# Spreading a column of maxima over all rows: one fp32 matmul, or three bf16 matmuls over the words of its bits

## The chip, the cores and the metric

The kernel runs on one core of a Trainium2 chip. The metric is the device time of one execution in microseconds (us): the median of several runs. Beside the runs there is one profiled execution of the kernel before, with a trace of every instruction; its span and its waits are what this document reads.

Five engines work side by side, each on its own list of instructions in order: TensorE (PE, with its weight loads on PEld), VectorE (DVE), ScalarE (ACT), GpSimd (POOL) and SyncE (SP), which issues the transfers.

## The reference

Linear attention over 8 batches, 8 heads, 576 positions and head size 64, and then a gated feed-forward network with an RMS norm over the 4608 tokens of width 512:

```python
def _attn_ref(q, k, v):
    q_s = softmax of q over the head dimension          # exp(q - max), over its sum
    k_s = k - np.max(k, axis=2, keepdims=True)          # maximum over the 576 positions
    k_s = np.exp(k_s)
    k_s = k_s / (np.sum(k_s, axis=2, keepdims=True) + 1e-09)
    kv = np.einsum('bhsd,bhse->bhde', k_s, v)
    return np.einsum('bhsd,bhde->bhse', q_s, kv)

def _moe_ref(x, w_gate, w_val, w_out, rms_g):           # x: 4608 x 512
    xn = x / rms * rms_g
    g = xn @ w_gate                                     # 512 x 1536
    return (g * sigmoid(g) * (xn @ w_val)) @ w_out
```

What matters here is the maximum of k over the positions: 64 numbers for each batch and head, or 128 for each pair of heads. There are 8 batches and 4 pairs, so 32 such columns of 128 maxima.

## The kernel before

The tokens are done in nine blocks of 512. The attention of later blocks runs between the matrix products of the feed-forward network of earlier ones. The order of all work is written out by hand: a string `ORDER` holds some 3000 steps such as `k_max.5.2` or `pp.3.1.6`; a loop calls the function of each name with its numbers, and each engine gets its instructions in the order in which these calls issue them. There is no scheduler behind it. A letter after a colon (`:D`, `:A`, `:P`) chooses the engine of a step that can run on several.

For a batch `b` over 0 and a pair of heads `g`, the steps around the change are these.

- `kd_load` fetches k with the head dimension in the partitions (`kd`, 128 x 576), and `k_max` (DVE, L548) reduces it to a column `kx` of 128 maxima, one in each partition.
- `k_rows` (PE, L560) makes a 128 x 128 tile in PSUM whose every row holds the 128 maxima: the column `kx`, repeated 128 times, is the stationary operand, and the identity matrix `ident` is the moving one, both fp32. The trace shows an fp32 matmul as two passes, each with a weight load of its own (28 matmuls of this kind are 56 records).
- `k_sub` (DVE, L565) subtracts that tile from k with the positions in the partitions (`kt`), and `k_exp` (ACT, L573) takes the exponential.
- `k_mm` (PE, L600) multiplies it by v: ten fp32 matmuls of 64 x 65, which are 20 records.
- `k_eps`, `k_rec`, `kv_hi`, `kv_lo` (DVE, DVE, ACT, DVE; L628, L631, L388, L651) divide by the sums and split the result into two parts for `q_x` (PE, L796).

For batches 2 to 7, one step `k_seg` holds two of these: it takes one PSUM bank (pool `ps_a`, two banks), does `k_mm` of one pair of heads and then `k_rows` of the next, so that on PE the ten matmuls of L600 stand straight ahead of the one of L560. There are 25 such steps; the first has only `k_rows`, the last only `k_mm`. For batch 1 the four `k_rows` stand alone. For batch 0 the maxima are used along the partitions (`k_exp` takes them as its bias), and nothing is spread.

The rest of PE's work is the feed-forward network, with weights and activations split into two halves: `pp` (L1166, f16, 256 columns each), `fu` and `f2` (L1214 and L1301, mostly f16, 512 columns), `f1` and `f1p` (L1230 in fp32r words, 512 columns; L1246 in f16). `ev` (L1181, L1184, L1187, L1190 and copies in L383) empties their PSUM banks on DVE and ACT. `fill` and `warm` (L476, L470) are matmuls on constants that keep PE busy; the weights of L476 are one bf16 zero in each partition, repeated 128 times.

Of the kernel before, what the change touches and what calls it, by code (L numbers as in the profile page):

```python
# [40 lines left out]
conv_low.2.0.2 q_x0.0.1 k_load.1.1 q_max0.1.0 q_t0.0.2 x_sq.0.1 x_hi.0.1:D q_load0.1.1 q_sub0.1.0:P q_c0.0.2:A
n_sum0.1 x_lo.0.1 q_load0.1.2 v_ones.1.0 q_exp.1.0 q_x0.0.2 k_sub.1.0 k_load.1.2 v_ones.1.1 f1.0.1.0.1 q_sum0.1.0
conv_mul.1.1 f1.0.1.0.3 f1.0.0.0.1 load_w.5.0 f1.0.0.0.3 x_hi.0.2:D x_sq.0.2 k_exp.1.0 conv_shift.1.1 fill.1 n_sum0.2
conv_sign.1.1 f1.0.1.0.2 f1.0.0.0.2 conv_low.0.2.1 f1.0.0.1.0 x_lo.0.2 f1.0.1.1.0 w_hi.1.0.2:P load_w.5.1 f1.0.1.1.1
conv_mul.0.2 f1.0.0.1.1 k_max.1.1 n_sum0.3 conv_low.4.0.2 conv_shift.0.2 kd_load.1.2 f1.0.0.1.2 f1.0.0.1.3 f1.0.1.1.2
conv_sign.0.2 f1.0.0.2.0 f1.0.1.1.3 w_lo.1.1:P f1.0.1.2.0 f1.0.1.2.1 n_t.0 conv_mul.2.0 load_w.4.2 f1.0.1.2.2
f1.0.0.2.1 f1.0.0.2.2 n_y0.0 conv_one.2.0 w_lo.1.0:P f1.1.0 conv_shift.2.0 n_y1.0 conv_mul.2.1 conv_sign.2.0:P
load_w.6.0 conv_low.5.0.2 f1.0.1.2.3 conv_shift.2.1 f1.0.0.2.3 k_mm.1.0 conv_sign.2.1 f1.1.1 v_load.1.2 n_cols.0
w_hi.2.0.2:A load_w.6.1 k_load.1.3 k_max.1.2 conv_low.4.2.1 w_lo.2.0:P q_max0.1.1 kd_load.1.3 conv_mul.1.2 n_rows.0
q_sub0.1.1:P g_mul.0 conv_shift.1.2 f1.2.0 w_lo.2.1:P silu.0 conv_sign.1.2 conv_low.6.0.2 v_ones.1.2 h_mul.0  # L50
# [25 lines left out]
v_ones.1.3 h_lo.5:P n_sq.1.0 n_col.0.1 w_hi.9.0.2:A h_lo.6:P k_mm.1.2 n_max.0.1 k_rows.1.3 n_sq.1.1 k_eps.1.2
v_load.2.0 f1.8.0 k_rec.1.2 w_lo.9.1:P k_sub.1.3 k_load.2.1 kv_norm0.1.2:A k_exp.1.3 n_bits.0.1.0 q_eps0.1.3
q_rec0.1.3 w_lo.9.0:P k_mm.1.3 g_mul.8 q_mul0.1.3:P silu.7 q_t0.1.1 k_eps.1.3 k_rec.1.3 f1.8.1 silu.8 q_c0.1.1:D
kv_norm0.1.3:A h_mul.7 n_bits.0.1.1 n_bits.0.1.2 n_bits.0.1.5 w_sc.0.1 n_bits.0.1.3 n_bits.0.1.4 q_x0.1.1 h_mul.8
w_hi.10.0.2:P b_hi.0.2:A n_col.1.0 w_sc.0.0 k_max.2.0 f1.9.0 n_max.1.0 kd_load.2.1 x_sq.1.1 x_raw.1.1:D b_lo.0.2:P  # L80
# [5 lines left out]
q_sub.2.0:D o_hi.9:A f2.8 h_lo.9:D x_sq.1.3 o_lo.9:D x_raw.1.3:A x_acc.1.3:D n_bits.1.3.1 n_hi.1:A t_op.0.1:P f2.9
k_max.2.1 o_hi.10:A n_lo.1:D kd_load.2.2 n_bits.1.3.3 o_lo.10:P q_exp.2.0 n_sum.1 q_sum.2.0 o_hi.11:A t_op.0.2:P
k_seg.0 q_half2.2.0 f1.10.0 n_t.1 v_ones.2.1 o_lo.11:P n_y0.1 n_y1.1 t_op.0.3:P f1.10.1 t_lo.0.0:P g_mul.10 n_rows.1
silu.10 t_hi.0.1:P q_half.2.1 f1.11.0 h_mul.10 x_nrm.1.1:P k_max.2.2 h_hi.10:A k_sub.2.0 kd_load.2.3 h_lo.10:P
# [1293 lines left out]
```

## Time and profile before

| what | value |
|---|---|
| runs before | 933.83 us median of 3 (933.64 to 934.41) |
| the profiled execution | 932.69 us, span 930.9 us from the first to the last instruction |
| PE | 913.8 us busy, 98% of the span |
| DVE | 617.3 us, 66% |
| ACT | 559.1 us, 60% |
| POOL | 305.9 us, 33% |
| granted TensorE clock | 1.0 |

A page of the profile gives the busy time of each engine, and the chain of work that ended last: from the last instruction back to whatever released it, or to the instruction before it on its engine. Matmuls are pipelined and overlap in the records, so "busy" for PE means that some matmul is under way, not that none waits; the steps from one start to the next say more than the durations. A line number (L560) is a line of the kernel before.

### The profile page before, as it was taken

How to read it: one execution, taken by the hardware profiler on the slowest of the kernel's cores; microseconds unless marked ns; L12 is line 12 of the kernel's file. 1: busy time of each engine (PE TensorE's matmuls, PEld its weight loads, DVE VectorE, ACT ScalarE, POOL GpSimd, SP SyncE). 2: the span in 40 equal slices, each digit the busy share in tenths (PEclk: the TensorE clock that was granted, in tenths of full speed). 3: DMA queues.
4: the chain of work that ended last, by engine and by line, in shares of the span. 5: the costliest groups of instructions: out<-in, count | busy, mean ns of one | idle time of the engine just before them, and what ended most of it. 6: DMA issues, size and time to landing. Idle time of an engine off the chain costs nothing.

```text
span 930.9 us, 16383 instructions
## 1 busy us (share of the span) xinstructions
PE 913.8 (98%) x6479; PEld 644.0 (69%) x6479; DVE 617.3 (66%) x1330; ACT 559.1 (60%) x880; POOL 305.9 (33%) x304
## 2 busy tenths in 40 slices
...
GB/s 342 360 265 226 61 53 38 36 23 188 54 53 131 33 42 24 110 94 53 66 117 77 65 53 29 36 51 1 38 35 23 1 2 46 1 1 24 23 1 46
DMA packets 29550, 68.06 MB, mean 73 GB/s; under 512 B 3744, under 2 KB 4000, under 8 KB 29472
## 3 DMA queue, kind: packets, MB, share of 16 engines
...
q14 instruction: 27, 0.22, 0.1%
HBM read 57.55 MB, written 9.44 MB: 72 GB/s over the span
## 4 chain that ended last, share of the span: by engine, by line
PE 83%; DVE 6%; ACT 4%; DMA 3%; issue 2%; POOL 1%; SPq 0%; ACTq 0%; POOLq 0%; DVEq 0%
PE ps_gv L1166 38%; PE ps_o L1214 22%; PE ps_o L1301 5%; PE ps_gv L1230 5%; PE ps_gv L1246 4%; PE ps_a L796 2%; PE ps_a L600 2%; DMA qt<-in_q_dram 1%; PE ps_a L560 1%; DMA w_gv<-in_kt_dram 1%; DMA w_br<-in_w_dram 1%; PE ps_a L1021 1%; ACT w_gv L388 0%; PE ps_a L725 0%; DVE x_raw L827 0%
## 5 line engine op out<-in xcount | busy, mean ns | idle before, releaser
L1166 PEld LDWEIGHTS <-w_gv 128*128 128x128 f16 x2016 | 196.0, 98 | 39.7 <-issue 3.2
L1166 PE MATMUL ps_gv<-xo,w_gv 128*128 128x256 f16 x1296 | 155.8, 273 | 0.6 <-ACT w_br L383 0.4
L1166 PE MATMUL ps_gv<-x_op,w_gv 128*128 128x256 f16 x720 | 86.5, 273 | 0.2
L1166 PEld LDWEIGHTS <-w_br 128*128 128x128 f16 x756 | 73.7, 98 | 14.3 <-issue 1.3
L1214 PEld LDWEIGHTS <-hh 128*128 128x128 f16 x504 | 48.9, 98 | 49.8 <-issue 0.4
L1214 PEld LDWEIGHTS <-hl 128*128 128x128 f16 x504 | 49.0, 98 | 47.5 <-issue 0.6
L1214 PE MATMUL ps_o<-w_o,hl 128*128 128x512 f16 x336 | 79.9, 379 | 0.0
L1214 PE MATMUL ps_o<-w_o,hh 128*128 128x512 f16 x336 | 78.4, 379 | 0.0
L1230 PE MATMUL ps_gv<-xo,wf 128*128 128x512 f32 x264 | 66.7, 404 | 0.0
L1166 PE MATMUL ps_gv<-xo,w_br 128*128 128x256 f16 x540 | 66.1, 273 | 0.0
L1230 PEld LDWEIGHTS ps_gv<-xo,wf 128*128 128x128 f32 x264 | 49.0, 188 | 12.9 <-issue 2.8
L1166 PEld LDWEIGHTS <-wf 128*128 128x128 f16 x504 | 49.2, 98 | 8.1 <-issue 0.3
L1181 DVE TENSOR_TENSOR tm<-ps_gv,tm 128x512 f32<-128x512 f32 x29 | 20.0, 689 | 50.9 <-PE ps_gv L1166 47.7
L785 POOL TENSOR_TENSOR ql<-qT,qh 128x512 fp32r<-128x512 f32 x14 | 18.2, 1301 | 87.1 <-ACT qh L383 87.1
L383 ACT COPY ps_gv<-ps_gv 128x512 f32<-128x512 f32 x42 | 24.0, 572 | 36.3 <-PE ps_gv L1166 13.8
L1181 DVE TENSOR_TENSOR w_br<-ps_gv,w_br 128x512 f32<-128x512 f32 x29 | 20.0, 690 | 37.4 <-PE ps_gv L1166 36.8
L1166 PE MATMUL ps_gv<-xo,wf 128*128 128x256 f16 x360 | 43.9, 273 | 0.0
L897 POOL TENSOR_TENSOR acc<-acc,sq 128x512 f32<-128x512 f32 x11 | 14.0, 1270 | 71.8 <-ACT sq L893 71.8
L1246 PE MATMUL ps_gv<-x_op,w_br 128*128 128x512 f16 x144 | 31.9, 379 | 0.0
L383 ACT COPY w_br<-ps_gv 128x512 f32<-128x512 f32 x29 | 17.0, 585 | 23.5 <-PE ps_gv L1166 23.4
L970 POOL TENSOR_TENSOR wf<-w_gv,wf 128x512 fp32r<-128x512 f32 x22 | 28.1, 1293 | 6.7 <-ACT wf L383 6.3
L383 ACT COPY tm<-ps_gv 128x512 f32<-128x512 f32 x29 | 17.0, 585 | 21.5 <-PE ps_gv L1166 21.3
...
## 6 DMA issues: line engine op xcount, KB each, us to landing
...
```

The source lines that it names most:

```text
L383: (e.copy if e is nc.scalar else e.tensor_copy)(dst, src)
L600: nc.tensor.matmul(ps[h * D:(h + 1) * D, :n1], lhsT=ke[:n, h, j], rhs=vt_[b, g][:n, j, h], start=(j == 0), stop=(j == len(rows) - 1))
L785: on(nc.gpsimd).tensor_tensor(out=ql, in0=qT_[j, g], in1=qh_[j, g][0].bitcast(F32), op=ALU.subtract)
L796: nc.tensor.matmul(px[:, c0:c1], lhsT=wt, rhs=mv[:, c0:c1], start=(i == 0), stop=(i == 2))
L897: on(nc.gpsimd).tensor_tensor(out=acc_[j], in0=acc_[j], in1=sq_[j, g], op=ALU.add)
L970: on(nc.gpsimd).tensor_tensor(out=cut(wl[:, a]), in0=W(s, a), in1=cut(wh[:, a].bitcast(F32)), op=ALU.subtract)
L1166: nc.tensor.matmul(pair(ps, i), lhsT=a[:, wt], rhs=y if i else y.rearrange("p (a c) -> p a c", a=2), start=(first and k == 0 and i == 0 an ...
L1181: nc.vector.tensor_tensor(out=v, in0=bank[j, u, 5 if n == 5 else 3], in1=v, op=ALU.add)
L1214: nc.tensor.matmul(po[2 * n + t], lhsT=a[:, o:o + P], rhs=w, start=(u == 0 and i == 0 and p == 0), stop=(u == NU - 1 and i == 1 and p == 2))
L1230: nc.tensor.matmul(pd[s], lhsT=m[:, a, c * P:(c + 1) * P], rhs=X[j, c][x], start=(n == 1), stop=(n == 3 * NKT))
L1246: nc.tensor.matmul(pd[s], lhsT=w[:, wt], rhs=x, start=(c == 0 and p == 0), stop=(c == NKT - 1 and p == 2))
L1301: nc.tensor.matmul(po[t], lhsT=a[:, t * P:(t + 1) * P], rhs=w, start=(i == 0 and n == 0), stop=(i == NF - 1 and n == len(terms) - 1))
```

## The change

`kx` becomes three columns instead of one. A new step `k_split`, called straight after `k_max` for each batch over 0, forms two remainders on DVE: the second column is the first less the number that its own upper 16 bits make as a bf16 word, and the third is the second less the upper word of the second. `upper` reads every other 16-bit word of an fp32 tile, starting with the second. `k_rows` then makes three matmuls that add up in the same PSUM tile: the upper words of each column, repeated 128 times, times the upper words of the identity, which are 1.0 and 0.0 in bf16. No other step is moved.

```diff
     def k_max(b, g):
-        kx_[b, g] = small.tile([P, 1], F32, name="kx")
-        nc.vector.tensor_reduce(out=kx_[b, g], in_=kd_[b, g], axis=AX.X, op=ALU.max, negate=b == 0)
+        t = small.tile([P, 3], F32, name="kx")
+        kx_[b, g] = [t[:, i:i + 1] for i in range(3)]
+        nc.vector.tensor_reduce(out=kx_[b, g][0], in_=kd_[b, g], axis=AX.X, op=ALU.max, negate=b == 0)
+
+    def upper(t):
+        return t.bitcast(BF16)[:, 1::2]
+
+    def k_split(b, g):
+        x = kx_[b, g]
+        for i in range(2):
+            nc.vector.tensor_tensor(out=x[i + 1], in0=x[i], in1=upper(x[i]), op=ALU.subtract)
...
     def k_rows(b, g, t=None):
         mb = (own(attn_ps(False)) if t is None else t)[:KP, P:2 * P]
-        nc.tensor.matmul(mb, lhsT=kx_[b, g].broadcast_to([P, KP]), rhs=ident, start=True, stop=True)
+        for i, x in enumerate(kx_[b, g]):
+            nc.tensor.matmul(mb, lhsT=upper(x).broadcast_to([P, KP]), rhs=upper(ident), start=i == 0, stop=i == 2)
...
-            nc.scalar.activation(kd_[b, g], kd_[b, g], AF.Exp, bias=kx_[b, g], accum_out=rs_[b, g])
+            nc.scalar.activation(kd_[b, g], kd_[b, g], AF.Exp, bias=kx_[b, g][0], accum_out=rs_[b, g])
```

In `ORDER`, 28 steps are added, each straight behind its `k_max` (the first and the last of them):

```diff
-v_load.1.1 kv_norm0.0.2:A k_max.1.0 w_hi.0.0.2:P
+v_load.1.1 kv_norm0.0.2:A k_max.1.0 k_split.1.0 w_hi.0.0.2:P
...
-kv_lo.6.3 k_max.7.3 pp.5.1.2
+kv_lo.6.3 k_max.7.3 k_split.7.3 pp.5.1.2
```

New lines shift the numbers: L560 of the kernel before is L574 after, L600 is L614, L1166 is L1180, L548 is L553, and the subtraction of `k_split` is L561.

What PE runs in one of the joint steps (`k_seg`, here the one that makes the rows of batch 3's last pair), between two products of the feed-forward network. Before (`vt` and `kt` are v and the exponentials of k, `w_gv` and `w_bx` weights):

```order
L1166 MATMUL ps_gv<-xo,w_gv 128x256
L600 MATMUL ps_a<-vt,kt 64x65 x10
L560 MATMUL ps_a<-ident,kx 128x128
L1166 LDWEIGHTS w_bx
L1166 MATMUL ps_gv<-xo,w_bx 128x2x128
```

After:

```order
L1180 MATMUL ps_gv<-xo,w_gv 128x256
L614 MATMUL ps_a<-vt,kt 64x65 x10
L574 LDWEIGHTS kx
L574 MATMUL ps_a<-ident,kx 128x128
L574 LDWEIGHTS kx
L574 MATMUL ps_a<-ident,kx 128x128
L574 LDWEIGHTS kx
L574 MATMUL ps_a<-ident,kx 128x128
L1180 LDWEIGHTS w_bx
L1180 MATMUL ps_gv<-xo,w_bx 128x2x128
```

One matmul in fp32, which loads its weights itself and runs in two passes, has become three pairs of weight load and matmul in bf16, in the same place.

What DVE runs around the maxima of batch 5, pair 2 (`qt` is a part of q, `x_raw` the attention's output). Before:

```order
L651 SCALAR_TENSOR_TENSOR kv_lo_113<-ps_a,rs,kv_hi_112 64x64 x2
L745 TENSOR_TENSOR st<-st,sw 128x16
L748 TENSOR_TENSOR qt<-qt,st 128x512
L548 TENSOR_REDUCE kx<-kd 128x1
L390 TENSOR_SCALAR x_raw<-ps_a,g_103 128x512
L897 TENSOR_TENSOR acc<-acc,sq 128x512
```

After:

```order
L665 SCALAR_TENSOR_TENSOR kv_lo_113<-ps_a,rs,kv_hi_112 64x64 x2
L759 TENSOR_TENSOR st<-st,sw 128x16
L762 TENSOR_TENSOR qt<-qt,st 128x512
L553 TENSOR_REDUCE kx<-kd 128x1
L561 TENSOR_TENSOR kx<-kx 128x1 x2
L394 TENSOR_SCALAR x_raw<-ps_a,g_103 128x512
L911 TENSOR_TENSOR acc<-acc,sq 128x512
```

Two subtractions of one element per partition stand between the maximum and the evacuation of `x_raw`, and each waits for the instruction before it, whose result it reads.

What DVE runs around the maxima of batch 1, pair 3, where the weights of the first blocks are put together from their words (L456 and L464, `w_o`). Before:

```order
L1269 TENSOR_TENSOR tm<-ps_o,tm 128x512
L548 TENSOR_REDUCE kx<-kd 128x1
L456 SCALAR_TENSOR_TENSOR ps_a<-ps_a,w_o 128x512
L464 SCALAR_TENSOR_TENSOR w_o<-w_o,ps_a 128x512
L565 TENSOR_TENSOR kt<-kt,ps_a 128x640
L694 TENSOR_REDUCE sm<-qt 128x8
```

After:

```order
L1283 TENSOR_TENSOR tm<-ps_o,tm 128x512
L553 TENSOR_REDUCE kx<-kd 128x1
L561 TENSOR_TENSOR kx<-kx 128x1 x2
L460 SCALAR_TENSOR_TENSOR ps_a<-ps_a,w_o 128x512
L468 SCALAR_TENSOR_TENSOR w_o<-w_o,ps_a 128x512
L579 TENSOR_TENSOR kt<-kt,ps_a 128x640
L708 TENSOR_REDUCE sm<-qt 128x8
```

Again the same order, with the two subtractions pushed in between. The lists of ACT, POOL and SP hold the same instructions in the same order as before.

More of the change, by code (lines that the diff above doesn't have):

```diff
@@ L41 @@
[L41 to L50, printed above, removed]
@@ L76 @@
[L76 to L80, printed above, removed]
@@ L86 @@
[L86 to L89, printed above, removed]
+k_tr0.1.0 v_load.1.0 kv_norm0.0.3:A k_tr0.1.1 conv_sign.0.1 n_sum0.0 v_load.1.1 kv_norm0.0.2:A k_max.1.0 k_split.1.0
@@ new lines @@
+w_lo.9.1:P k_sub.1.3 k_load.2.1 kv_norm0.1.2:A k_exp.1.3 n_bits.0.1.0 q_eps0.1.3 q_rec0.1.3 w_lo.9.0:P k_mm.1.3
+g_mul.8 q_mul0.1.3:P silu.7 q_t0.1.1 k_eps.1.3 k_rec.1.3 f1.8.1 silu.8 q_c0.1.1:D kv_norm0.1.3:A h_mul.7 n_bits.0.1.1
+n_bits.0.1.2 n_bits.0.1.5 w_sc.0.1 n_bits.0.1.3 n_bits.0.1.4 q_x0.1.1 h_mul.8 w_hi.10.0.2:P b_hi.0.2:A n_col.1.0
+w_sc.0.0 k_max.2.0 k_split.2.0 f1.9.0 n_max.1.0 kd_load.2.1 x_sq.1.1 x_raw.1.1:D b_lo.0.2:P b_hi.0.3:A b_hi.0.0:A
+x_acc.1.1:D n_sq.1.2 n_col.1.1 f1.9.1 b_lo.0.0:D v_ones.2.0 k_load.2.2 n_sq.2.2 n_max.1.1 w_lo.10.0:P g_mul.9 n_sq.2.0
@@ new lines @@
+b_lo.0.3:D q_t0.1.2 q_max2.2.0 w_lo.10.1:D n_sq.2.1 q_load.2.2 n_col.2.0 f2.5 t_op.0.0:D silu.9 n_max.2.0
+w_hi.11.0.2:P n_sq.3.0 h_mul.9 q_c0.1.2:D b_hi.0.1:A t_hi.0.0:A q_t0.1.3 b_lo.0.1:D n_col.2.1 h_hi.7:A v_load.2.1 f2.6
+n_max.2.1 w_lo.11.0:P n_sq.3.1 o_hi.7:A q_max.2.2 h_lo.7:P q_x0.1.2 o_lo.7:D h_hi.8:A o_hi.8:A w_lo.11.1:D f2.7
+x_sq.1.2 o_lo.8:D q_c0.1.3:A h_lo.8:D x_raw.1.2:A n_bits.1.3.0 x_acc.1.2:D q_x0.1.3 h_hi.9:A q_sub.2.0:D o_hi.9:A f2.8
+h_lo.9:D x_sq.1.3 o_lo.9:D x_raw.1.3:A x_acc.1.3:D n_bits.1.3.1 n_hi.1:A t_op.0.1:P f2.9 k_max.2.1 k_split.2.1
@@ new lines @@
+v_ones.2.2 q_load.3.0 k_rec.2.1 q_sub.2.2:P k_sub.2.2 kv_hi.2.1:A k_load.3.0 v_load.2.3 h_mul1.18 t_op.1.3:P k_exp.2.2
+k_max.3.1 k_split.3.1 q_exp.2.2 h_hi.18:P k_seg.3 kv_lo.2.1 kd_load.3.2 q_sum.2.2 q_x.2.0 h_lo.18:P k_load.3.1
+k_sub.2.3 silu1.19 v_load.3.0 f2.16 q_hi.2.1:A k_eps.2.2 q_half2.2.2 v_ones.2.3 t_op.2.1:P x_sq.2.0 q_half.2.3
+x_raw.2.0:A k_rec.2.2 q_max2.2.3 kv_hi.2.2:A q_sum2.2.2 q_rec.2.2 q_sub.2.3:P kv_lo.2.2 f2.17 q_max.3.0 q_mul.2.2:P
+k_max.3.2 k_split.3.2 q_exp.2.3 q_lo.2.1:P k_exp.2.3 kd_load.3.3 q_sum.2.3 q_x.2.1 q_half2.2.3 v_ones.3.0 t_op.2.2:P
@@ new lines @@
+q_t.2.2 k_seg.4 x_sq.2.1 q_half.3.0 q_load.3.1 t_op.2.3:P q_hi.2.2:A k_eps.2.3 f2.18 k_rec.2.3 v_load.3.1 k_sub.3.0
+x_raw.2.1:A k_load.3.2 q_lo.2.2:P kv_hi.2.3:A k_max.3.3 k_split.3.3 k_exp.3.0 kv_lo.2.3 kd_load.4.0 x_acc.2.1:P
+q_max.3.1 q_x.2.2 k_seg.5 q_sum2.2.3 v_ones.3.1 x_sq.2.2 q_rec.2.3 t_lo.0.3:P x_raw.2.2:D f1p.19.1 v_load.3.2
+k_eps.3.0 k_rec.3.0 q_mul.2.3:P k_sub.3.1 k_load.3.3 t_hi.1.0:A kv_hi.3.0:A k_max.4.0 k_split.4.0 x_acc.2.2:P
+k_exp.3.1 q_t.2.3 kd_load.4.1 f1p.20.0 h_mul1.19 t_lo.1.0:P q_hi.2.3:A q_load.3.2 kv_lo.3.0 h_hi.19:A q_lo.2.3:D
@@ L193 @@
-hu_lo.3.5.1:P k_rec.5.2 k_sub.5.3 kv_hi.5.2:A pp.4.0.2 ev.4.0.2 kv_lo.5.2 q_sum2.6.0 q_rec.6.0 q_mul.6.0:D pp.4.0.7
-ev.4.0.8 v_ones.6.0 k_max.6.2 pp.4.0.5 ev.4.0.3 kd_load.6.3 pp.4.0.4 ev.4.0.5 k_exp.5.3 pp.4.0.3 q_exp.6.1 q_sum.6.1
-q_x.5.2 ev.4.0.6 ev.4.0.9 k_seg.16 ev.4.0.10 x_sq.5.2 ev.4.0.11 pp.4.1.1 v_load.6.1 hu_hi.4.0.0 x_acc.5.2:D k_load.6.2
+kv_lo.4.2 pp.3.2.6 ev.3.2.8 q_max2.5.2 q_sub.5.2:D k_max.5.2 k_split.5.2 q_x.4.2 ev.3.2.2 v_ones.5.0 pp.3.2.5
+x_raw.4.2:D q_hi.4.3:A kd_load.5.3 x_sq.4.2 q_lo.4.3:P pp.3.2.7 x_acc.4.2:D fu.3.1.1.0 k_exp.4.3 q_t.5.0 ev.3.2.3
@@ new lines @@
+q_load.5.3 k_seg.12 q_exp.5.2 ev.3.2.5 q_sum.5.2 pp.3.2.3 v_load.5.1 k_eps.4.3 k_load.5.2 k_rec.4.3 k_sub.5.0
+kv_hi.4.3:A fu.3.1.1.1 ev.3.2.6 k_exp.5.0 ev.3.2.10 pp.3.3.1 v_ones.5.1 kv_lo.4.3 hu_hi.3.2.0 q_half2.5.2
+hu_lo.3.2.0:P fu.3.1.0.0 q_max.5.3 q_half.5.3 fu.3.1.0.1 q_sum2.5.2 q_rec.5.2 q_mul.5.2:D fu.3.2.0.0 q_max2.5.3
+q_sub.5.3:D k_max.5.3 k_split.5.3 q_exp.5.3 pp.3.2.4 q_sum.5.3 kd_load.6.0 q_x.4.3 q_half2.5.3 ev.3.2.9 fu.3.2.0.1
+q_sum2.5.3 x_raw.4.3:D x_sq.4.3 ev.3.2.11 ev.3.3.0 k_seg.13 x_acc.4.3:D hu_hi.3.2.1 pp.3.3.6 k_eps.5.0 k_load.5.3
@@ new lines @@
+o_x_lo.4.5:P q_hi.5.2:A pp.3.5.2 x_raw.5.1:D hu_lo.3.4.0:P q_max.6.1 pp.3.5.6 o_x_hi.4.6:A k_max.6.1 k_split.6.1
+q_lo.5.2:P ev.3.5.8 kd_load.6.2 fu.3.4.1.1 ev.3.5.2 o_x_lo.4.6:D pp.3.5.5 q_t.5.3 x_sq.5.1 q_max2.6.0 q_load.6.2
+x_acc.5.1:D pp.3.5.7 q_sub.6.0:D k_exp.5.2 fu.3.4.0.0 ev.3.5.3 q_exp.6.0 ev.3.5.5 fu.3.4.0.1 q_sum.6.0 q_half2.6.0
+pp.3.5.3 q_max.6.2 q_half.6.1 pp.3.5.4 ev.3.5.6 ev.3.5.10 pp.4.0.1 ev.3.5.9 q_max2.6.1 q_sub.6.1:D hu_hi.3.5.0
+k_seg.15 ev.3.5.11 ev.4.0.0 hu_lo.3.5.0:D hu_hi.3.5.1 pp.4.0.6 v_load.6.0 k_eps.5.2 k_load.6.1 hu_lo.3.5.1:P k_rec.5.2
@@ L298 @@
-fu.8.4.0.0 store.8.3 fu.8.4.0.1 fu.8.5.0.0 fu.8.5.0.1 store.8.0 store.8.1
+q_sum2.6.1 q_rec.6.1 q_mul.6.1:D q_x.5.3 k_max.6.3 k_split.6.3 q_exp.6.2 pp.4.1.4 ev.4.1.5 kd_load.7.0 x_sq.5.3
+q_sum.6.2 x_raw.5.3:A x_acc.5.3:P pp.4.1.3 q_half2.6.2 k_exp.6.0 q_half.6.3 fu.3.5.1.1 n_hi.5:A ev.4.1.6 n_lo.5:P
+store.3.2 pp.4.2.1 store.3.3 ev.4.1.10 n_sum.5 q_max2.6.3 hu_hi.4.1.0 q_sub.6.3:D k_seg.17 q_hi.6.0:A hu_lo.4.1.0:D
+q_exp.6.3 fu.4.0.0.0 v_load.6.2 n_t.5 q_lo.6.0:P k_load.6.3 n_y0.5 fu.4.0.1.0 n_y1.5 ev.4.1.9 fu.4.0.1.1 ev.4.2.0
@@ new lines @@
+pp.4.4.7 q_rec.7.0 k_max.7.1 k_split.7.1 v_ones.6.3 q_mul.7.0:P kd_load.7.2 q_x.6.1 ev.4.4.3 q_sum2.6.3 q_rec.6.3
+q_mul.6.3:D pp.4.4.4 q_hi.6.2:A q_max.7.1 x_raw.6.1:A q_lo.6.2:P q_half.7.1 fu.4.1.0.0 q_max2.7.1 q_t.6.3 q_sub.7.1:P
+fu.4.2.1.1 ev.4.4.9 q_load.7.2 ev.4.4.8 pp.4.4.5 pp.4.5.1 ev.4.4.5 q_exp.7.1 ev.4.4.11 pp.4.4.3 o_x_hi.5.5:A q_max.7.2
+hu_hi.4.4.1 o_x_lo.5.5:P q_sum.7.1 fu.4.1.0.1 ev.4.4.6 hu_lo.4.4.1:P q_half2.7.1 ev.4.5.0 k_seg.19 q_half.7.2
+hu_hi.4.3.0 ev.4.4.10 pp.4.5.6 k_load.7.1 v_load.7.0 hu_lo.4.3.0:D pp.4.5.2 k_eps.6.2 ev.4.5.2 k_rec.6.2 q_sum2.7.1
```

409 lines of the change are left out of this document (197 added, 212 removed).

## Prediction

> **What bounds the kernel now.** I read the busy shares on the page, then its chain of work, then that chain in order of time, and last the timeline of PE and DVE where the chain touches the changed lines.
>
> ```profile
> span 930.9 us, 16383 instructions
> PE 913.8 (98%) x6479; PEld 644.0 (69%) x6479; DVE 617.3 (66%) x1330; ACT 559.1 (60%) x880; POOL 305.9 (33%) x304
> PE 83%; DVE 6%; ACT 4%; DMA 3%; issue 2%; POOL 1%; SPq 0%; ACTq 0%; POOLq 0%; DVEq 0%
> PE ps_gv L1166 38%; PE ps_o L1214 22%; PE ps_o L1301 5%; PE ps_gv L1230 5%; PE ps_gv L1246 4%; PE ps_a L796 2%; PE ps_a L600 2%; DMA qt<-in_q_dram 1%; PE ps_a L560 1%; DMA w_gv<-in_kt_dram 1%; DMA w_br<-in_w_dram 1%; PE ps_a L1021 1%; ACT w_gv L388 0%; PE ps_a L725 0%; DVE x_raw L827 0%
> ```
>
> PE is the bound: 83% of the chain that ended last is its work, and DVE has only 6%. The changed matmul, L560, holds 1% of the chain. So PE time saved there should come off the end, unless something else is late. Where L560 lies on the chain, in order of time (start, us, what):
>
> ```profile
> 30.18 0.49 PE ps_a L560 x2
> ...
> 55.49 0.50 PE ps_a L560 x2
> ...
> 105.01 0.22 PE ps_a L560 x2
> ...
> 110.84 0.42 PE ps_a L560 x2
> ...
> 143.49 0.22 PE ps_a L560 x2
> ...
> 220.04 0.42 PE ps_a L560 x2
> ...
> 664.56 0.42 PE ps_a L560 x2
> ```
>
> From 220.04 to 664.56 there are 18 such pieces, each of 0.42 or 0.43 us and each behind L600 in a joint step; with the one at 110.84 that makes 19 alike. Two of 0.22 us stand behind other matmuls. Five of the 28 are not on the chain (it runs over DVE, ACT or POOL there), and I count nothing for these.
>
> **The price of L560 now.** Timeline of PE (start, us, line, shapes): a joint step, the last joint step, which has no L560, and a place where L476 comes straight behind L600.
>
> ```profile
> 279.41 0.95 PE L600 MATMUL ps_a<-vt,kt 128*64 128x65 f32 x20
> 280.29 0.49 PE L560 MATMUL ps_a<-ident,kx 128*128 128x128 f32 x2
> 280.61 1.48 PE L1166 MATMUL ps_gv<-xo,w_bx 128*128 128x256 f16 x12
> ...
> 676.04 0.95 PE L600 MATMUL ps_a<-vt,kt 128*64 128x65 f32 x20
> 676.92 1.25 PE L1214 MATMUL ps_o<-w_o,hh 128*128 128x512 f16 x5
> ...
> 12.23 0.95 PE L600 MATMUL ps_o<-w_gv 128*64 128x64 f32 x20
> 13.11 0.82 PE L476 MATMUL ps_gv<-ones_b,zero_b 128*128 128x512 bf16 x3
> ```
>
> From L600's start to the next product's start it is 1.20 us with L560 (279.41 to 280.61) and 0.88 without (676.04 to 676.92). L560 costs 0.32 us. The third place shows that weights made of one repeated bf16 word start behind L600 in the same 0.88 us as ordinary f16 weights: the repetition costs nothing. How long such an uncovered 16-bit weight load holds up a matmul is in the spread of L476's durations (min/median/max):
>
> ```profile
> L476 PE MATMUL ps_gv<-ones_b,zero_b x20: 378/379/391, 11.7 to 35.0; 128*128 128x512 bf16 x20
> ```
>
> 391 less 379 is 0.012 us, paid once, by the first matmul of a run.
>
> **The price of three bf16 matmuls.** No 16-bit matmul of 128 columns is in the trace. The chain gives the steps of the wider ones and of fp32r words:
>
> ```profile
> 143.71 8.19 PE ps_gv L1230 x36
> ...
> 275.55 3.93 PE ps_gv L1166 x36
> ...
> 291.23 3.88 PE ps_o L1214 x18
> ```
>
> 256 columns take 3.93 / 36 = 109 ns and 512 take 3.88 / 18 = 216 ns, with a weight load ahead of each. That is 0.416 ns a column and about 3 ns fixed; carried on to 128 columns it gives 56 ns, the lower end. The upper end is 109 ns, if 128 columns cost what 256 do, because of the weight load, or because the words of `ident` lie 4 bytes apart. Against the second: L1230 reads 4 bytes for each column and takes 8.19 / 36 = 228 ns for 512, hardly more than f16. I take 56, nearest to both rows.
>
> So a joint step takes 0.88 + 0.012 + 3 x 0.056 = 1.06 us instead of 1.20: 0.14 us less. Nineteen of them give 2.66 us. Behind other matmuls the weight load is covered: 0.22 becomes 0.17, twice, 0.10 us. Together 2.76 us.
>
> [...]
>
> **What DVE pays.** Each `k_split` is two subtractions of one element per partition, each waiting for the one before. The nearest rows are such a pair, and the two places where the delay reaches the chain:
>
> ```profile
> 398.28 0.16 DVE L628 TENSOR_SCALAR rs<-ps_a 128x1 f32<-128x1 f32 x1 [0.34 <-PE ps_a L560]
> 398.47 0.17 DVE L631 RECIPROCAL rs<-rs 128x1 f32<-128x1 f32 x1
> ...
> 401.54 0.74 DVE L548 TENSOR_REDUCE kx<-kd 128x1 f32<-128x576 f32 x1
> ...
> 402.32 0.75 DVE L390 TENSOR_SCALAR x_raw<-ps_a,g 128x512 f32<-128x512 f32 x1
> 403.10 0.60 ACT L893 ACTIVATE sq<-ps_a 128x512 f32<-128x512 f32 x1 [0.93 <-DVE x_raw L390]
> ...
> 405.80 0.95 PE L600 MATMUL ps_a<-vt,kt 128*64 128x65 f32 x20 [0.30 <-ACT kt L573]
> ```
>
> A dependent step is 0.19 us (398.28 to 398.47), so two put off the next DVE instruction by about 0.38 us (0.30 if the next one overlaps the second, 0.42 with both waits in full); 28 of them are 10.6 us more on an engine with 314 us idle. Nearly all of it is covered: in the closest case PE wants the words 7 us later (23.20 below to 30.18 above), and DVE soon waits for someone anyway. At 401.54 it isn't: `x_raw` starts at the end of the maximum, ACT waits for it, and PE then idles 0.30 us at L600 for ACT's exponential. There 0.37 us go on the end.
>
> In the first 80 us the chain jumps between engines:
>
> ```profile
> 23.20 0.74 DVE L548 TENSOR_REDUCE kx<-kd 128x1 f32<-128x576 f32 x1
> 24.22 0.69 DVE L383 COPY x_raw<-ps_o 128x512 f32<-128x512 f32 x1 [0.28 <-PE ps_o L712]
> ...
> 56.89 0.74 DVE L548 TENSOR_REDUCE kx<-kd 128x1 f32<-128x576 f32 x1
> 57.55 0.69 DVE L456 SCALAR_TENSOR_TENSOR ps_a<-ps_a,w_o 128x512 int32<-128x512 int32 x1
> ...
> 59.86 0.69 DVE L694 TENSOR_REDUCE sm<-qt 128x8 f32<-128x512 f32 x1 [0.17 <-ACT qt L752]
> ```
>
> At 23.20 there are 0.28 us idle behind the maximum, so 0.1 us of the 0.38 is left over. At 56.89 only the 0.17 us idle at 59.86 takes some up: 0.21 us are left, and the saving at 55.49, which comes to ACT, is lost behind them. The one at 30.18 counts, 0.14 us as in a joint step. Together the first stage is 0.1 + 0.21 - 0.14 = 0.17 us longer. The maxima at 37 and 45 us lie ahead of a DVE stretch that waits for a transfer; I cost them at nothing, at worst 0.2 each.
>
> **The sum.** -2.76 + 0.37 + 0.17 = -2.2 us. The profiled execution took 932.69 us, 1.8 more than its span; it becomes 930.5. The median of the runs, 933.83, stands 1.1 us above it, so I expect 933.83 - 2.2 = **931.6 us**.
>
> **Rivals.**
>
> *The short matmul is not short.* Between 56 and 109 ns the middle is 82: then a joint step saves 0.062 us, 19 of them 1.18; 0.05 are lost at the two 0.22 us places and 0.62 to DVE's delays (0.37, 0.1, 0.21, less 0.06 at 30.18); 0.5 us remain, 933.3. At 109 ns nothing is saved (0.02 lost in each joint step, 0.1 at each short place), 0.6 in all, and DVE's delays of 0.7 come on top: 935.1. Against it: both slopes above. For it: no row has 128 columns. Chance 0.17, most of it at 82.
>
> *The saving is absorbed.* PE gains on the others, and where it meets one that doesn't gain, it waits. Such stretches on the chain:
>
> ```profile
> 254.97 1.51 POOL qt L770
> 257.42 5.06 DMA qt<-in_q_dram
> ...
> 497.92 1.76 DVE hl L1202
> ```
>
> Both stretches begin at PE's own work (they follow the sum of squares of a block), so they should move along with it; but if half of the 2.76 us were lost before such places, 933.0 would be left. Chance 0.19.
>
> *Slower, because DVE is late.* Between 200 and 570 us DVE is busy some 80% of the time, and it empties the PSUM banks that PE fills.
>
> ```profile
> 500.00:560.00 60.00, 48.76 (x117) 1.00 0.19 56
> ...
> L1166 PE MATMUL ps_gv<-x_op,w_br 128*128 128x256 f16 x216 | 26.5, 273 | 0.3 <-DVE w_br L1181 0.2
> ```
>
> The first row is DVE's busy time in a window (48.76 of 60 us), the second a group of PE's products with what its idle time waited for (0.3 us, 0.2 of it for DVE). If DVE were just in time with the banks, each `k_split` behind which it has no idle 0.38 us would stop PE for that long. On DVE's timeline I count 11 of the 24 from 118 us on, the first and the last of them:
>
> ```profile
> 150.23 0.74 DVE L548 TENSOR_REDUCE kx<-kd 128x1 f32<-128x576 f32 x1
> ...
> 526.47 0.69 DVE L548 TENSOR_REDUCE kx<-kd 128x1 f32<-128x576 f32 x1
> ```
>
> That is 11 x 0.38 = 4.2 us, and 933.83 - 2.2 + 4.2 = 935.8. It breaks even at 6 places. Against it: PE waited for DVE in only 0.2 us of these 26.5. Chance 0.12.
>
> **Chances and range.** The forecast has 0.52; its own range is 930.9 (no delay of DVE on the end: 933.83 - 2.76 - 0.14) to 932.4 (two more delays of DVE on it). A measurement of this kernel can tell about 0.2%, 1.9 us, from no change: faster means below 931.96. Of the forecast 0.46 lies below that, 0.06 above; the absorbed case and the long matmuls are almost all "same", with 0.02 on the fast side; DVE late ends slower or just within. Faster 0.48, same 0.41, slower 0.11. The range takes in the absorbed case and the matmul of 82 ns, and leaves out DVE late and the 109 ns; at both ends it leaves room for the spread of the runs before, 0.8 us: 930.3 to 934.6.
>
> **What would show it.** In the profile after, L574 should have 84 matmuls, and from L614's start to the next product's start in a joint step 1.06 us; 1.14 means 82 ns, 1.22 means 109. DVE should have 56 rows at L561, and the step from `k_max` to the next instruction should grow from 0.66 to 1.04 us. At 405.80 PE's idle time ahead of L614 should be 0.3 to 0.4 us longer. If PE's idle time behind DVE's lines L1195 to L1204 (`ev` after) grows by more than 2 us, the third rival holds; if L574's steps are short and the end does not move, the second.

## The result and the profile after

The changed kernel takes 945.29 us, the median of 6 runs (940.0 to 947.41), against 933.74 us for 6 runs of the kernel before (932.8 to 934.41). The ratio is 1.0115, with a 95% interval of 1.0090 to 1.0141: 1.15% slower, about 11 us, where 2.2 us less were forecast. The profiled execution took 945.60 us.

First the page: span, busy times, and the chain of work that ended last, by engine.

```profile
span 943.8 us, 16483 instructions
PE 916.8 (97%) x6502; PEld 643.4 (68%) x6507; DVE 637.6 (68%) x1386; ACT 560.1 (59%) x880; POOL 307.1 (33%) x304
...
PE 80%; DVE 8%; DMA 4%; ACT 4%; issue 2%; POOL 1%; SPq 0%; ACTq 0%; POOLq 0%; DVEq 0%
```

DVE has 20.3 us more to do, where 28 pairs at 0.38 us make 10.6. Its share of the chain rose from 6% to 8%.

PE's part looks as it should. A joint step in the timeline (start, us, line, shapes, count), the one that stood at 279.41 before:

```profile
292.63 0.95 PE L614 MATMUL ps_a<-vt,kt 128*64 128x65 f32 x20
293.51 0.34 PE L574 MATMUL ps_a<-ident,kx 128*128 128x128 bf16 x3
293.69 1.03 PE L1180 MATMUL ps_gv<-xo,w_bx 128*128 128x256 f16 x8
```

From L614's start to the next product it is 1.06 us, as forecast, 0.14 less than before.

The subtractions are another matter. All records of line L561: durations in ns, min/median/max.

```profile
L561 DVE TENSOR_TENSOR kx<-kx x56: 158/160/1264, 24.3 to 585.9; 128x1 f32<-128x1 f32 x56
```

One element in each partition takes 0.16 us in the median, and up to 1.26. Over 0.158 us apiece the 56 have 15.0 us in all. What a long pair looks like, with POOL beside it (timeline, DVE and POOL):

```profile
37.57 0.74 DVE L553 TENSOR_REDUCE kx<-kd 128x1 f32<-128x576 f32 x1
...
38.18 2.53 POOL L984 TENSOR_TENSOR wf<-w_gv,wf 128x512 fp32r<-128x512 f32 x2
38.35 2.37 DVE L561 TENSOR_TENSOR kx<-kx 128x1 f32<-128x1 f32 x2
40.65 0.68 DVE L460 SCALAR_TENSOR_TENSOR ps_a<-ps_a,w_br 128x512 int32<-128x512 int32 x1
```

POOL runs two instructions of 1.28 us, and each of the two subtractions begins 0.1 to 0.2 us after one of them and ends with it. So it is in the whole trace: 21 of the 56 last over 0.17 us, each began while POOL was running an instruction that reads SBUF, and each ended 13 to 20 ns after that one ended. Of the 35 short ones four lay beside such an instruction that went on for longer than themselves: three had begun 12 to 60 ns ahead of it, and one 5 ns behind it.

The kernel before had such rows already, in its records of two small DVE lines of the same kind and size:

```profile
L763 DVE SCALAR_TENSOR_TENSOR sm<-sm,sw x28: 134/175/1023, 153.2 to 715.3; 128x16 f32<-128x16 f32 x28
...
L941 DVE SCALAR_TENSOR_TENSOR ps_a<-y,ps_a x27: 168/178/180, 41.7 to 808.8; 128x16 f32<-128x16 f32 x27
```

L763 reads two tensors in SBUF and has 134 to 1023 ns: six of the 28 last over 0.2 us, and each of the six began while POOL was running such an instruction and ended 31 to 34 ns after it. L941 reads one of its two from a tile of the PSUM pool and never goes over 180, though 17 of its 27 lie beside a POOL instruction. The prediction took its price from L628 and L631, which read one tensor.

What becomes of the delay (timeline, DVE and PE):

```profile
48.41 1.38 DVE L561 TENSOR_TENSOR kx<-kx 128x1 f32<-128x1 f32 x2
49.70 0.68 DVE L699 TENSOR_REDUCE st<-qt 128x8 f32<-128x512 f32 x1
50.30 0.70 DVE L961 STREAM_TRANSPOSE r<-y 128x512 f32<-128x512 f32 x1
51.10 0.69 DVE L1276 TENSOR_TENSOR tm<-ps_gv,r 128x512 f32<-128x512 f32 x1
...
51.94 0.47 PE L1244 MATMUL ps_gv<-xo,wf 128*128 128x512 f32 x1 [2.23 <-DVE tm L1276]
```

DVE runs with hardly a gap from 33 us on (busy for 18.20 of the 19 us up to 52), so the delay of two long pairs arrives in full at L1276 (51.10 us, 47.53 before: 3.6 us later), which empties the PSUM bank that PE's next product needs. Before, L1230 ran through there; now PE stands for 2.23 us. At 86.38 it stands for 2.45 us (0.45 before), at 243.87 for 1.19 us, there for the transfer of `kt`. A long pair is behind that wait too, by way of SyncE's list (timeline, DVE and SP):

```profile
235.61 2.05 DVE L561 TENSOR_TENSOR kx<-kx 128x1 f32<-128x1 f32 x2
...
239.01 0.71 DVE L789 STREAM_TRANSPOSE qT<-qt 128x512 f32<-128x512 f32 x1
239.75 0.33 SPq L686 DMA_DIRECT2D qt<-in_q_dram  x1
...
240.64 0.38 SPq L522 DMA_DIRECT2D kt<-in_k_dram  x1
```

The transfer of `qt` is issued when the transpose L789 has ended, and that of `kt` stands behind it in the list. The transpose starts 4.2 us after the start of its maximum instead of 2.2, and `kt` is issued only 3.2 us before the product that waits for it starts.

And behind each of these three waits the products run at half pace (behind the first, those of L1244 start 427 ns apart, and some 232 ns apart afterwards). Windows (length, busy us of PE, PEld, DVE, ACT, POOL, and then the granted clock):

```profile
50.00:60.00 10.00, 8.06 (x29) 6.20 (x30) 8.35 (x18) 6.80 (x12) 4.45 (x6) 0.83 0.59 215
...
86.00:92.00 6.00, 5.62 (x17) 4.18 (x18) 5.63 (x14) 4.04 (x7) 3.56 (x4) 0.72 0.68 220
...
243.00:248.00 5.00, 4.13 (x30) 2.28 (x31) 4.71 (x13) 2.44 (x6) 3.82 (x5) 0.66 0.62 195
```

The missing clock is 0.17 x 10, 0.28 x 6 and 0.34 x 5: 1.7 us each time, which is some 3.4 us at half the clock. Everywhere else it is 1.00; in the profiled execution before it was 1.00 throughout.

Up to 105 us the changed kernel falls 8.2 us behind, at 160 us another 0.9, between 220 and 295 us another 4, and 1.4 at 420. From there the joint steps win 1 us back.

### The profile page after: what moved, and what is told of

It is laid out like the page before. It is cut to its first block, busy times and chain, and to the rows that moved or that the text cites. A ratio compares the mean times of both kernels' runs of the same rounds, so it can differ in the third digit from the quotient of the medians.

```text
span 943.8 us, 16483 instructions
## 1 busy us (share of the span) xinstructions
PE 916.8 (97%) x6502; PEld 643.4 (68%) x6507; DVE 637.6 (68%) x1386; ACT 560.1 (59%) x880; POOL 307.1 (33%) x304
## 4 chain that ended last, share of the span: by engine, by line
PE 80%; DVE 8%; DMA 4%; ACT 4%; issue 2%; POOL 1%; SPq 0%; ACTq 0%; POOLq 0%; DVEq 0%
PE ps_gv L1180 38%; PE ps_o L1228 22%; PE ps_gv L1260 5%; PE ps_o L1315 5%; PE ps_gv L1244 4%; PE ps_a L614 2%; PE ps_a L810 2%; DMA w_gv<-in_w_dram 2%; DMA w_br<-in_w_dram 1%; DVE kt L579 1%; DVE kx L561 1%; PE ps_a L574 1%; DMA g_sb<-in_rms_g_dram 1%; DVE ps_a L460 1%; PE ps_a L1035 0%
## 5 line engine op out<-in xcount | busy, mean ns | idle before, releaser
L1180 PEld LDWEIGHTS <-w_gv 128*128 128x128 f16 x2016 | 195.7, 98 | 40.1 <-issue 3.8
L1180 PE MATMUL ps_gv<-xo,w_gv 128*128 128x256 f16 x1296 | 155.9, 273 | 0.7 <-ACT w_br L387 0.5
L1180 PE MATMUL ps_gv<-x_op,w_gv 128*128 128x256 f16 x720 | 86.5, 273 | 0.3 <-ACT wf L387 0.3
L1180 PEld LDWEIGHTS <-w_br 128*128 128x128 f16 x756 | 73.6, 98 | 14.4 <-issue 1.3
L1244 PE MATMUL ps_gv<-xo,wf 128*128 128x512 f32 x264 | 70.1, 419 | 2.2 <-DVE tm L1276 2.2
L1180 PE MATMUL ps_gv<-xo,w_br 128*128 128x256 f16 x540 | 66.1, 273 | 0.0
L1244 PEld LDWEIGHTS ps_gv<-xo,wf 128*128 128x128 f32 x264 | 51.1, 196 | 16.5 <-issue 5.4
L1180 PEld LDWEIGHTS <-wf 128*128 128x128 f16 x504 | 49.2, 98 | 8.1 <-issue 0.3
L1195 DVE TENSOR_TENSOR tm<-ps_gv,tm 128x512 f32<-128x512 f32 x29 | 20.0, 689 | 49.7 <-PE ps_gv L1180 47.1
L1195 DVE TENSOR_TENSOR w_br<-ps_gv,w_br 128x512 f32<-128x512 f32 x29 | 20.0, 690 | 36.3 <-PE ps_gv L1180 35.9
L1180 PE MATMUL ps_gv<-xo,wf 128*128 128x256 f16 x360 | 43.9, 273 | 0.0
L614 PEld LDWEIGHTS ps_a<-vt,kt 128*64 128x64 f32 (+1 forms) x560 | 21.1, 137 | 15.8 <-issue 6.3
L614 PE MATMUL ps_a<-vt,kt 128*64 128x65 f32 (+1 forms) x560 | 26.9, 232 | 4.6 <-ACT kt L587 2.1
```

What stands on the lines that cost most here:

```text
L614: nc.tensor.matmul(ps[h * D:(h + 1) * D, :n1], lhsT=ke[:n, h, j], rhs=vt_[b, g][:n, j, h], start=(j == 0), stop=(j == len(rows) - 1))
L1180: nc.tensor.matmul(pair(ps, i), lhsT=a[:, wt], rhs=y if i else y.rearrange("p (a c) -> p a c", a=2), start=(first and k == 0 and i == 0 an ...
L1195: nc.vector.tensor_tensor(out=v, in0=bank[j, u, 5 if n == 5 else 3], in1=v, op=ALU.add)
L1244: nc.tensor.matmul(pd[s], lhsT=m[:, a, c * P:(c + 1) * P], rhs=X[j, c][x], start=(n == 1), stop=(n == 3 * NKT))
```

## The experiments

The theory: a DVE instruction that reads two tensors in SBUF waits for POOL's running instruction; that holds up DVE's queue, then PE, and then the clock falls. Rival 1: two more dependent instructions are themselves too many for DVE's queue. Rival 2: the bf16 matmuls or the clock do it, without DVE.

**One tensor instead of two.** Label e1.

```diff
-            nc.vector.tensor_tensor(out=x[i + 1], in0=x[i], in1=upper(x[i]), op=ALU.subtract)
+            nc.vector.tensor_scalar(out=x[i + 1], in0=x[i], scalar1=upper(x[i]), scalar2=None, op0=ALU.subtract)
```

> The three words and their place stay; each subtraction becomes a TENSOR_SCALAR that reads one tensor (the word) and takes the upper half as its per-partition scalar, instead of a TENSOR_TENSOR that reads two tensors in SBUF. Theory (two-tensor reads wait for POOL's running instruction): no subtraction lasts over 0.4 us (with two tensors 0.16 to 1.26), the wait of 2.2 us at 51.9 us is gone, the granted clock is 1.00 everywhere, and the recorded sum of -2.2 us comes true: 931 to 933 us. Rival 1 (two more dependent instructions in DVE's queue are themselves too many in the first stage): 943 to 947 us as with two tensors. Rival 2 (the bf16 matmuls or the clock do it): 943 to 947 us too.

Measured: 932.73 us, ratio 0.9993 (0.9983 to 1.0003). The records of L561, and the place at 38 us:

```profile
L561 DVE TENSOR_SCALAR kx<-kx x56: 211/214/217, 24.3 to 573.2; 128x1 f32<-128x1 f32 x56
```

```profile
38.59 2.56 POOL L984 TENSOR_TENSOR wf<-w_gv,wf 128x512 fp32r<-128x512 f32 x2
38.76 0.47 DVE L561 TENSOR_SCALAR kx<-kx 128x1 f32<-128x1 f32 x2
39.14 0.69 DVE L460 SCALAR_TENSOR_TENSOR ps_a<-ps_a,w_br 128x512 int32<-128x512 int32 x1
...
81.63 0.84 PE L739 MATMUL ps_a<-qT,ot 128*128 128x64 f32 x3 [1.89 <-DVE w_gv L460]
```

With the same count, order and dependence, beside the same POOL instruction, no subtraction is held: 211 to 217 ns, though 27 of the 56 lie wholly within a POOL instruction. The wait at 51.9 us is gone and so are 1.2% of the time. Both rivals fall. The recorded -2.2 us did not come: the ratio says -0.7 (-1.6 to +0.3). The pair puts the next instruction off by 0.50 us, not 0.38 (38.64 would be the next start, 0.66 behind the maximum; it is 39.14), and PE stands 1.89 us at 81.63 us, 1.44 more than before; most of that is not the subtractions', since e3 below, which has none, stands there for 1.41 us.

**DVE's part alone, PE's part alone.** In e2 the split stays and `k_rows` is the fp32 matmul of before; in e3 the three bf16 matmuls stay and the subtractions are gone.

```diff
 # e2
-        for i, x in enumerate(kx_[b, g]):
-            nc.tensor.matmul(mb, lhsT=upper(x).broadcast_to([P, KP]), rhs=upper(ident), start=i == 0, stop=i == 2)
+        nc.tensor.matmul(mb, lhsT=kx_[b, g][0].broadcast_to([P, KP]), rhs=ident, start=True, stop=True)
 # e3: no k_split, and
+        for i in range(3):
+            nc.tensor.matmul(mb, lhsT=upper(kx_[b, g][0]).broadcast_to([P, KP]) if i == 0 else zero_b.broadcast_to([P, KP]),
+                             rhs=upper(ident), start=i == 0, stop=i == 2)
```

> DVE's part alone: the two subtractions stay behind each maximum, with two tensors in SBUF, but the rows are spread by the one fp32 matmul as before the change (the split words are not used). Theory and rival 1 (the loss is DVE's): the 11.5 us are lost and the 2.8 us of PE not saved, 946 to 950 us. Rival 2 (the loss comes with the bf16 matmuls): 933 to 936 us.

> PE's part alone: three bf16 matmuls of the same shapes, but no subtraction; the first takes the upper half of the maximum, the second and third a column of zeros, so the lower bits of the maximum are left out (the same shift stands in numerator and denominator). Theory and rival 1: only PE's saving is left, 0.14 us at 19 places and 0.1, that is 933.8 - 2.8 = 931.0, between 930 and 932; clock 1.00. Rival 2: 943 us or more.

Measured: e2 946.73 us, ratio 1.0130 (1.0116 to 1.0144); e3 932.13 us, ratio 0.9981 (0.9972 to 0.9989). The whole loss comes with the split. PE's part gives -1.8 us by its ratio instead of -2.8, and the time lies just outside the 930 to 932 us expected. In its profiled execution the joint steps save what they should, but the wait of 1.41 us for DVE named above takes 0.96 us of it, and a new wait 1.08 us:

```profile
246.55 0.49 PE L933 MATMUL ps_a<-ql,mean_w 128*128 128x512 f32 x1 [1.08 <-DVE ql L919]
```

That is the second rival of the prediction, in a small part; why DVE is late at these two places without any subtraction was not followed up.

**One word.** A common shift cancels in a softmax, so the lower bits of the maximum may be left out. In e4 `k_split` is gone and one matmul is left:

```diff
+        nc.tensor.matmul(mb, lhsT=upper(kx_[b, g][0]).broadcast_to([P, KP]), rhs=upper(ident), start=True, stop=True)
```

> One bf16 matmul of the maximum's upper half, no subtraction; the maximum's lower bits are left out. Theory: a joint step falls from 1.20 to 0.88 + 0.012 + 0.058 = 0.95 us, 0.25 us at 19 places and 0.16 at two: 933.8 - 5.1 = 928.7, between 927.5 and 930. If PE's time at these places were not on the path, 933 to 934. Rival 2 (any bf16 matmul there is harmful): above 936.

Measured: 928.91 us, ratio 0.9943 (0.9931 to 0.9956), the fastest of all. The joint step of its timeline (276.80 to 277.75 us) is 0.95 us, as forecast:

```profile
276.80 0.95 PE L611 MATMUL ps_a<-vt,kt 128*64 128x65 f32 x20
277.68 0.23 PE L571 MATMUL ps_a<-ident,kx 128*128 128x128 bf16 x1
277.75 0.49 PE L1177 MATMUL ps_gv<-xo,w_bx 128*128 128x256 f16 x3
```

**Where the loss sits.** e5 reads two tensors for `b == 1` and one for the rest; e6 the other way round.

```diff
-            nc.vector.tensor_tensor(out=x[i + 1], in0=x[i], in1=upper(x[i]), op=ALU.subtract)
+            if b == 1:      # e6: b > 1
+                nc.vector.tensor_tensor(out=x[i + 1], in0=x[i], in1=upper(x[i]), op=ALU.subtract)
+            else:
+                nc.vector.tensor_scalar(out=x[i + 1], in0=x[i], scalar1=upper(x[i]), scalar2=None, op0=ALU.subtract)
```

> The changed kernel; the four splits of the first stage (b = 1) read two tensors in SBUF, the other 24 one (TENSOR_SCALAR). Theory: the eight early subtractions wait for POOL and PE stands at 51.9 and 86.4 us as in the changed kernel. Up to 82 us the changed kernel stood 8.2 us behind the kernel before, the one-tensor form 1.9: 932.7 + 6.3 = 939, between 937 and 941, with the granted clock down to half for some us after each of the two waits. If the loss were spread over all splits in proportion to their count, 4 of 28 would give 932.7 + 1.8 = 934.5.

> The opposite: the first four splits read one tensor, the 24 later ones two. Theory: the first 100 us as in the one-tensor form, then the late waits of the changed kernel (161, 230, 242, 244 with its drop of the clock, 420 us): 945.3 - 6.3 = 939, between 937 and 941. By count of splits 932.7 + 10.8 = 943.5.

Measured: e5 935.97 us, ratio 1.0034 (1.0014 to 1.0054); e6 938.59 us, ratio 1.0053 (1.0034 to 1.0071). For e6 the forecast by places holds. e5 came out lower, and its ten runs say why: they go from 933.62 to 941.32 us. The five with a mean granted clock of 0.999 or more over the whole run took 933.6 to 935.5 us, the three with 0.995 or 0.996 took 939.9 to 941.3. Its profiled execution is one of the first kind:

```profile
52.12 2.08 PE L1247 MATMUL ps_gv<-xo,wf 128*128 128x512 f32 x8 [2.23 <-DVE tm L1279]
```

```profile
50.00:60.00 10.00, 7.84 (x32) 5.69 (x33) 9.76 (x19) 7.52 (x13) 4.98 (x6) 1.00 0.62 224
```

The wait is the same, 2.23 us, and the clock does not fall behind it. My 939 us had taken the fall for granted.

**Another place.** The splits of groups 1 and 2 of the first stage are issued later, where POOL stood still in the kernel before (50.1 to 54.9 us).

```diff
-... f1.0.0.1.1 k_max.1.1 k_split.1.1 n_sum0.3 ... k_load.1.3 k_max.1.2 k_split.1.2 conv_low.4.2.1 ...
+... f1.0.0.1.1 k_max.1.1 n_sum0.3 ... k_load.1.3 k_max.1.2 conv_low.4.2.1 ...
-... g_mul.1 f1.2.1 conv_shift.3.0
+... g_mul.1 k_split.1.1 k_split.1.2 f1.2.1 conv_shift.3.0
```

> The changed kernel with all splits on two tensors, but those of groups 1 and 2 of the first stage are issued later, both behind the DVE product that stood at 50.1 us before, ahead of a conversion that waits for ACT; POOL ran nothing from 50.1 to 54.9 us. Theory: these four subtractions then last 0.16 us each, PE's wait of 2.2 us at 51.9 us and the half clock behind it go, and 3 to 5 us of the 11.5 come back: 940 to 942. If the instruction count or the dependent waits were the cause, the place would not matter: 945.

Measured: 937.91 us, ratio 1.0053 (1.0036 to 1.0070). More came back than expected (timeline, DVE and PE):

```profile
48.88 4.47 PE L1244 MATMUL ps_gv<-xo,wf 128*128 128x512 f32 x19
```

```profile
50.71 0.61 DVE L561 TENSOR_TENSOR kx<-kx 128x1 f32<-128x1 f32 x4
52.13 0.70 DVE L460 SCALAR_TENSOR_TENSOR ps_a<-ps_a,w_gv 128x512 int32<-128x512 int32 x1 [0.80 <-ACT ps_a L449]
```

The four subtractions that had taken 3.75 us now take 0.61 together, DVE waits for ACT behind them anyway, and PE runs through. Place decides, because it decides what POOL is doing.

**On POOL.** `nc.gpsimd.tensor_tensor` instead of `nc.vector.tensor_tensor`.

> The same subtractions with two tensors, issued on POOL instead of DVE, so that they stand in POOL's own queue and never wait for a running POOL instruction of another queue. Theory: DVE runs as in the kernel before, the rows come later by POOL's current work (1 to 3 us) but are wanted some us later: 931 to 934, if POOL's two extra instructions do not hold up its conversions; where they do by 0.3 us each in the first stage, 934 to 936. If the split as such were the cause, 943 or more.

Measured: 934.02 us, ratio 1.0007 (0.9995 to 1.0019), neither gain nor loss. The subtractions take 193 ns in the median there, but in the profiled execution PE still waits for DVE at L739, for 2.38 us, and the clock from 82 to 90 us is 0.79:

```profile
81.74 1.41 PE L739 MATMUL ps_a<-qT,ot 128*128 128x64 f32 x4 [2.38 <-DVE w_gv L460]
```

**The clock by itself.** e9 leaves DVE as in the changed kernel and gives PE products with zeros to do while it waits; e10 is the changed kernel once more beside it.

```diff
-f1.1.1 v_load.1.2 ...
+f1.1.1.0.0 f1.1.1.0.1 ... f1.1.1.2.2 fill.9 f1.1.1.2.3 v_load.1.2 ...
-... h_mul.3 q_x0.1.0 ...
+... h_mul.3 fill.10 q_x0.1.0 ...
```

> The changed kernel as it is (two-tensor splits on DVE), but PE gets products with zeros into an open bank where it waited: 9 of 512 columns ahead of the last product of the block that ended at 49.7 us, 10 ahead of L739 at 84 us (216 ns each, 1.9 and 2.2 us). DVE's work and its delays stay. Theory (the wait itself is DVE's, but a third of the loss is the granted clock, halved for 3.4 us behind a wait): the waits shrink to what the products leave, the clock stays at 1.00 from 50 to 95 us, 1.7 us come back for each of the two places and perhaps 1 more of what follows: 940 to 942. If the halved clock has nothing to do with PE standing still, it is still there and the time is 944 to 947, or more by what the products delay.

> The changed kernel once more, beside the filled one on the same chip: 943 to 947 us, and the lower of its runs those with the higher mean granted clock (0.998 against 0.994 was 940.0 against 947.4).

> The filled kernel again, for a trace: its first profiled execution lasted 1987 us, with every product of PE at half pace from the first, and shows nothing of the two places. Theory: PE's remaining waits at 52 and 84 us are below 1 us, the granted clock is 1.00 from 50 to 95 us, 940 to 942 us. If the clock halves there although PE is busy, its drop does not come from PE standing still.

Measured: e9 941.09 us in five executions, ratio 1.0070 (1.0054 to 1.0085), without a sixth of 1987.08 us; e11 940.12 us, ratio 1.0073 (1.0055 to 1.0091); e10 942.78 us, ratio 1.0095 (1.0073 to 1.0116). The intervals overlap, so the gain of the fill is not clear of the noise. The nine runs of the filled kernel lie between 939.62 and 941.99 us, the twelve of the changed one between 939.47 and 947.41.

The profiled execution of e10 is the best evidence of all. It is the same program as the one shown above and took 939.47 us, 6.1 less. Its wait, and its windows:

```profile
52.10 1.17 PE L1244 MATMUL ps_gv<-xo,wf 128*128 128x512 f32 x4 [2.24 <-DVE tm L1276]
```

```profile
50.00:60.00 10.00, 7.90 (x32) 5.67 (x33) 9.76 (x20) 7.55 (x13) 5.14 (x6) 1.00 0.61 220
84.00:90.00 6.00, 6.00 (x22) 3.64 (x21) 5.57 (x14) 5.57 (x10) 4.00 (x5) 1.00 0.80 291
238.00:243.00 5.00, 3.92 (x37) 2.27 (x38) 4.79 (x13) 2.10 (x6) 3.92 (x6) 1.00 0.65 200
```

The wait of 2.24 us is there, the fall of the clock is not. Of the 12.9 us by which the first profiled execution (945.60) stood over the one before (932.69), 6.8 are there at full clock; 5.1 are the three stretches at half clock (3 x 1.7), and about 1 is a wait for ACT at 283.40 us, which lasts 1.81 us there, 1.65 before and only 0.68 in e10. In the trace of e11 the fill stands in the wait:

```profile
49.54 2.13 PE L480 MATMUL ps_o<-ones_b,zero_b 128*128 128x512 bf16 x9
51.32 0.58 PE L1244 MATMUL ps_o<-xo,wf 128*128 128x512 f32 x1
52.12 1.17 PE L1244 MATMUL ps_gv<-xo,wf 128*128 128x512 f32 x4 [0.22 <-DVE tm L1276]
```

```profile
50.00:60.00 10.00, 9.78 (x41) 6.43 (x40) 9.76 (x20) 7.56 (x13) 5.12 (x6) 1.00 0.64 220
84.00:90.00 6.00, 6.00 (x23) 3.84 (x22) 4.74 (x12) 4.67 (x9) 3.14 (x4) 1.00 0.77 278
```

L1244 starts at 52.12 us as without the fill (52.10): DVE decides, PE's zeros change nothing in that, and the clock stays at 1.00. At 84 us the ten zero products run past the wait: L739 starts at 83.85 us instead of 83.16. One trace cannot prove that the fill holds the clock there, since e10 was at 1.00 without one. The narrow spread of the nine runs speaks for it, and so do the windows of the clock in the last section, where PE stood for 1.45 to 2.45 us ahead of each of the three at half clock; that two of the nine still had a mean clock of 0.997 fits the waits that were left unfilled (1.2 us at 240), which I did not test.

## Why the prediction was wrong

**PE's part was right in its prices.** 84 matmuls at L574, a joint step of 1.06 us, and in e4 two matmuls fewer save another 0.11. At 82 ns apiece, the middle of the prediction's range, the joint step would have been 1.14 us; the three took 0.18 us together (293.51 to 293.69). Of the 2.76 us only 1.8 reached the end in e3.

**What DVE pays: the price failed.** The step "two put off the next DVE instruction by about 0.38 us (0.30 ... 0.42)" took rows that read one tensor for instructions that read two. The pair cost 0.38 to 2.4 us, according to what POOL was running; 15.0 us over the 56 came on top. All 21 subtractions over 0.17 us ended 13 to 20 ns after the POOL instruction during which they began, and e1 and e7 bear it out: with one tensor they last 211 to 217 ns beside the same POOL instruction, and with two, where POOL stands still, four take 0.61 us together. The rows of L763 above (134 to 1023 ns) show the same by themselves, and the prediction did not weigh them.

**"I cost them at nothing" failed too.** The maxima at 37 and 45 us were said to lie ahead of a DVE stretch that waits for a transfer. DVE hardly waits between 33 and 52 us (busy for 17.03 of these 19 us before, 18.20 after), and what arrives late is `r` and with it the bank of `ps_gv`. For the whole first stage 0.17 us were forecast. ACT's table load at L752, at 104.47 us before, comes 8.2 us later in the first execution after, 3.4 in e10 with the clock at 1.00, 1.9 in e1 with the short subtractions, and 0.9 in e3 with none. So the two added instructions as such are worth about 1 us there, their waits for POOL 1.5 more, and the two stretches of half clock with what follows them 4.8 more: an estimate, from one execution of each kernel.

**At 401.54 us the mechanism was right and the size wrong.** I had 0.37 us; the chain of the trace after (timeline):

```profile
414.78 1.26 POOL L799 TENSOR_TENSOR ql<-qT,qh 128x512 fp32r<-128x512 f32 x1 [0.99 <-ACT qh L387]
414.85 1.40 DVE L561 TENSOR_TENSOR kx<-kx 128x1 f32<-128x1 f32 x2
416.28 0.75 DVE L394 TENSOR_SCALAR x_raw<-ps_a,g 128x512 f32<-128x512 f32 x1
417.07 0.60 ACT L907 ACTIVATE sq<-ps_a 128x512 f32<-128x512 f32 x1 [2.37 <-DVE x_raw L394]
...
418.97 0.74 ACT L587 ACTIVATE kt<-kt 128x640 f32<-128x640 f32 x1
...
419.76 0.95 PE L614 MATMUL ps_a<-vt,kt 128*64 128x65 f32 x20 [1.73 <-ACT kt L587]
```

The pair took 1.40 us because POOL began 0.07 us earlier, and PE's wait grew from 0.30 to 1.73 us: 1.43. With the short pair of e1 it is 0.80 us.

**The rival of the late DVE had the right sign and the wrong place.** It let PE wait behind the lines that empty the banks of the later blocks (L1195 to L1204). Those waits did not grow: the group that had 0.3 us of idle time, 0.2 of it for DVE, still has. The loss sits in the first stage, at 160 us, in the step from 220 to 250 us, and at 420.

**A term was missing: the clock.** No rival let a wait cost more than its own length. Here a wait of 1.2 to 2.5 us cost up to 1.7 us more.

By ratio, each known to some 0.2%, e5 and e6 stand 0.41% and 0.60% above e1. Their sum, 1.01%, is the whole difference of e10 to e1 (1.02%); of the first result (1.22%) 0.2% are left, which lie within the spread of the clock.
